# Four key blocks of a pair's scores in one session, and the norm's scale on GpSimd

## The chip, the cores and the metric

The kernel runs on one core of one Trainium2 chip. The metric is the device time of one execution in microseconds; of several runs, the median. A profile comes from one further execution on the chip.

## What is computed

Attention with normalized queries and keys over 8 batches, 12 heads, 448 positions and 64 elements a head, then a mixer on its output: a low-rank mix over the positions (rank 32) and an MLP of width 3072 over 768 channels, each added to its input.

```python
def _attn_ref(q, k, v, g_q, g_k):
    def rmsnorm(x, g):
        rms = np.sqrt(np.mean(x * x, axis=-1, keepdims=True) + 1e-06)
        return x / rms * g
    q_n, k_n = (rmsnorm(q, g_q), rmsnorm(k, g_k))
    scores = np.matmul(q_n, k_n.transpose(0, 1, 3, 2)) / np.sqrt(q.shape[-1])
    scores = scores - np.max(scores, axis=-1, keepdims=True)
    attn = np.exp(scores)
    attn = attn / (np.sum(attn, axis=-1, keepdims=True) + 1e-09)
    return np.matmul(attn, v)

def _moe_ref(x, U, V, w_ch1, w_ch2):
    xt = x.transpose(0, 2, 1)
    h = xt @ U @ V
    u = x + h.transpose(0, 2, 1)
    ch = np.maximum(u @ w_ch1, 0.0) @ w_ch2
    return u + ch
```

The result must agree with this; the matmuls take bf16.

## The kernel before

**Pairs.** Two heads make a pair, and there are 48 pairs, p = 0 to 47, six to a batch. Two pairs make a load (t = p // 2). The 448 positions lie as 112 partitions by four blocks. One step of a pair goes through these stages:

- `load` (L184) brings q and k of a load from HBM, on SP's DMA queue; `load_v` brings v.
- `squares` (L215, POOL) and `reduce` (L218, DVE) give the sums of squares, and `rsqrt` (L223 and L224, ACT: Ln, then Exp with the scale -0.5) turns them into 1/rms. They go to a PSUM bank of their own, `rs_bank`, from which `rs_of(p)` takes 16 columns by p % 6.
- `scale` (L229, DVE) multiplies q and k by 1/rms and writes bf16 `qkn`, of which there are three buffers.
- The scaled pair is turned. Up to pair 11 PE does it (`transposes`, L244), and DVE copies the result out of PSUM. From pair 12 on a DMA on SP's queue does it (`dma_transposes`, L262), and ACT multiplies the gains in afterwards (`gains`, L267).
- `scores(p, kcs)` (L276, PE) takes the four key blocks, kc = 0 to 3. Each is two matmuls of 64 rows by 448 columns, one for each head, on the two halves of the array's rows; they start within a few nanoseconds of each other and write to two PSUM banks. A run of such matmuls with nothing else between is called a session here.
- `expo(p, kc)` (L281, ACT) takes the exponential of one key block of both heads, 112 x 896, from PSUM into SBUF (`E`).
- `values(p, hh)` multiplies `E` by v (L289, 16 matmuls of 65 columns), and DVE divides by the row sum into x.

**Mixer.** `mixing(b)` is the low-rank part: `mix_t` (L336 into `pm`, L345 out of it) and `mix_x` (L359 to L362 into `px`, L364 out of it), then DMA transposes into `u`. `mlp(b)` is a generator. Its first half computes 24 chunks `ph` (L392, six matmuls each), with a relu after each on ACT (L395) or DVE (L397): from batch 1 on, every third chunk is DVE's. Its second half computes `po` (L416, 24 matmuls that add up in one bank), and DVE adds x (L420). Even batches have 384 columns in a chunk `ph`, odd ones 512.

**Order.** A long `head` does the first batch's attention from a list written out by hand (`HEAD`). After it the MLP of batch b is woven with the attention of batch b + 1. `attention(b)` gives a list of pieces, each with a weight; `weave` runs the MLP's generator until the share of its work that the weights ask for is done, then issues the piece. PE, ACT, DVE, POOL and SP's queue each execute in the order in which this issues. Before pair 12 (`early`), `scale(p + 1)` is issued in pair p; from then on `scale(p + 2)`, with its DMA transposition.

**PSUM.** There are eight banks: three for tiles with the tag "mm" (`ph`, `po`, `o`, `px`, `pm`, `pt`), two times two for `sc`, and one for `rs_bank`. A tile of a pool waits for the readers of the one whose bank it takes.

The lines that issue the scores of one pair, in `attention`:

```python
            add(2 if 6 < p <= 12 else 1, scores, p, (0, 1))
            add(0, expo, p, 0)
...
            alone = p >= 12 and p % 6 == 0
            add(0 if alone else 1, expo, p, 1)
...
            add(2 if alone else 1, scores, p, (2, 3))
...
            add(0, expo, p, 2)
...
            add(0 if early else 1, expo, p, 3)
```

Of the kernel before, what the change touches and what calls it, by code (L numbers as in the profile page):

```python
# [9 lines left out]
FP32 = mybir.dt.float32  # L10
BF16 = mybir.dt.bfloat16
AX = mybir.AxisListType.X
AF = mybir.ActivationFunctionType
# [4 lines left out]
def kernel(  # L18
# [13 lines left out]
    nc = tc.nc  # L32
    B, H, S, D = q.shape
# [5 lines left out]
    P = 128  # L39
    NJ = 4  # L40
    SP = S // NJ
# [4 lines left out]
    PAD = 64  # L46
# [15 lines left out]
    consts = ctx.enter_context(tc.tile_pool(name="consts", bufs=1))  # L62
    norm = ctx.enter_context(tc.tile_pool(name="norm", bufs=2))
    upool = ctx.enter_context(tc.tile_pool(name="upool", bufs=1))
    opool = ctx.enter_context(tc.tile_pool(name="opool", bufs=3))
    ps_mm = ctx.enter_context(tc.tile_pool(name="ps_mm", bufs=3, space=bass.MemoryType.PSUM))
    ps_s = ctx.enter_context(tc.tile_pool(name="ps_s", bufs=2, space=bass.MemoryType.PSUM))
    ps_r = ctx.enter_context(tc.tile_pool(name="ps_r", bufs=1, space=bass.MemoryType.PSUM))

    shift = consts.tile([P, 3 * P], BF16, name="shift")  # L70
    ident = shift[:, P:2 * P]
# [16 lines left out]
    NE, NV, NQ, NWARM = 2, 3, 4, 12  # L88
    Es = [consts.tile([SP, 2, PAD + NJ * S + PAD], BF16, name=f"E{i}") for i in range(NE)]
# [7 lines left out]
    qkL = [consts.tile([P, 2, 2, 2, NJ * D], FP32, name=f"qk{i}") for i in range(2)]  # L97
    vL = [consts.tile([P, HG, NJ * D], FP32, name=f"vt{i}") for i in range(2)]

    rs_bank = ps_r.tile([SP, 6 * 16], FP32, name="rs_bank")  # L100

    def rs_of(p, n=1, of=rs_bank):

        c = 16 * (p % 6)
        return of[:, c:c + 16 * n]

    spare = hT.rearrange("p k n -> p (k n)").bitcast(FP32)

# [64 lines left out]
    sqs, qkns, scs, t4s, us, begun = {}, {}, {}, {}, {}, {}  # L173
# [43 lines left out]
    def reduce(p, hs=ALL):  # L217
        nc.vector.tensor_reduce(rs_of(p, of=sums).rearrange("p (s h j) -> p s h j", s=2, h=2)[:, :, hs],  # L218
                                sqs[p].rearrange("p (s h j d) -> p s h j d", s=2, h=2, d=D)[:, :, hs], AX, OP.add)

    def rsqrt(p, n=1):
        rs = rs_of(p, n)
        nc.scalar.activation(rs, rs_of(p, n, sums), AF.Ln, bias=eps)  # L223
        nc.scalar.activation(rs, rs, AF.Exp, scale=-0.5)  # L224

    def scale(p):
        t, a = divmod(p, 2)
        qkns[p] = norm.tile([SP, NJ, 4, D], BF16, tag="qkn", name="qkn", bufs=3)
        nc.vector.tensor_tensor(  # L229
            qkns[p].rearrange("p j g d -> p g j d"),  # L230
            qk_of[t][0:SP, a].rearrange("p s h (j d) -> p (s h) j d", d=D),
            rs_of(p).rearrange("p (g j) -> p g j ()", j=NJ).to_broadcast([SP, 4, NJ, D]),
            OP.mult)

    def k_side(p):

        return qkTs[3] if p == 0 else qkTs[p % NQ]

    def blocks(p):
        return qkTs[p % NQ][:, 0:SQK].rearrange("p (j s r) -> p j s r", j=NJ, s=2)  # L240
# [28 lines left out]
    def scores(p, kcs):  # L269
        flat, n = k_side(p), SP if p == 0 else P  # L270
        for kc in kcs:
            sc = ps_s.tile([P, 2, 512], FP32, tag="s", name="sc")
            c = (2 * kc + 1) * SP
            for hh in range(2):
                pp = slice(hh * D, (hh + 1) * D)
                nc.tensor.matmul(sc[0:n, hh, 0:S], flat[pp, c:c + n], blocks(p)[pp, :, 0],  # L276
                                 start=True, stop=True)
            scs[p, kc] = sc

    def expo(p, kc):  # L280
        nc.scalar.activation(Es[p % NE][:, :, PAD + kc * S:PAD + (kc + 1) * S], scs.pop((p, kc))[0:SP, :, 0:S],  # L281
                             AF.Exp, scale=float(D) ** 0.5)

    def products(p, hh, o):
        par, E, va, hl = p // 6 % 2, Es[p % NE], vas[(p // 2) % NV], 2 * (p % 2) + hh
# [145 lines left out]
    def attention(b):  # L431
        items = []

        def add(weight, fn, *args):
            items.append((weight, lambda: fn(*args)))

        for p in range(b * 6, b * 6 + 6):
            t, odd = divmod(p, 2)
            early = p < 12
            if p == 12:  # L440
                add(0, gains, p)
            add(2 if 6 < p <= 12 else 1, scores, p, (0, 1))
            add(0, expo, p, 0)
            if p == 11:
                add(0, touch, 7)
                add(0, load, 7)
                add(0, load_v, 7)
            elif early and odd:
                add(0, rsqrt, p + 1, 2)
                add(0, scale, p + 1)  # L450
            elif early and p > 6:
                add(0, scale, p + 1)
            elif p >= 12 and p + 2 < NP:
                add(0, scale, p + 2)
                add(0, dma_transposes, p + 2)
            alone = p >= 12 and p % 6 == 0
            add(0 if alone else 1, expo, p, 1)
            if p % 6:
                add(1, values, p - 1, 0)
            if t + 2 < NT:  # L460
                for a in range(2):
                    if odd and p > 11 or p == 11 and a == 0:
                        add(0, reduce, 2 * t + 4 + a if p > 11 else 12)
                    elif not odd and not early:
                        add(0, squares, 2 * t + 4 + a)
            add(2 if alone else 1, scores, p, (2, 3))
            if early and not odd:
                add(0.5, transposes, p + 1)
                if p < 10:
                    add(0, reduce, p + 2)  # L470
            add(0, expo, p, 2)
            if p % 6:
                add(1, values, p - 1, 1)
            if early and not odd:
                if p < 10:
                    add(0, reduce, p + 3)
                for a in range(2):
                    if p != 8:
                        add(0, squares, (10 if p == 6 else 12) + a)
            if odd and p > 11 and t + 3 < NT:  # L480
                add(0, load, t + 3)
                add(0, load_v, t + 3)
            if not odd and t + 1 < NT:
                add(0, cast_v, t + 1)
            if p + 1 < NP and p > 11:
                add(0, gains, p + 1)
            add(0 if early else 1, expo, p, 3)
            if early and odd and p < 11:
                add(1, transposes, p + 1)
            if p == 9:  # L490
                add(0, touch, 6)
                add(0, load, 6)
                add(0, load_v, 6)
            if odd and p > 11 and t + 2 < NT:
                add(0, rsqrt, 2 * t + 4, 2)
        add(1, values, b * 6 + 5, 0)
        add(1, values, b * 6 + 5, 1)
        return items
# [53 lines left out]

    def head():
        warm, rsb = (ps_s.tile([P, 2, 512], FP32, tag="s", name="sc") for _ in range(2))
        banks = [ps_mm.tile([P, 512], FP32, tag="mm", name=f"bank{i}") for i in range(3)]
        held = {}
        copies = {"a": nc.scalar.copy, "v": nc.vector.tensor_copy}
        rs0 = [rs_bank[:, 0:8], rsb[0:SP, 0, 0:8]]
        sums0 = [sums[:, 0:8], sums[:, 8:16]]
        FIRST, REST = slice(0, 1), slice(1, NJ)  # L560

# [11 lines left out]
        def op(name, p, n, how):  # L573
# [45 lines left out]
            elif name in ("Ek", "El"):  # L619
                js = slice(0, NJ) if p else FIRST if name == "Ek" else REST  # L620
                take_k(p, turned(("T" if p else "T" + name[1], p)), copies[how], js)
            elif name == "SC":
                scores(p, (n,))
            elif name == "X":
                expo(p, n)
# [35 lines left out]
        for word in HEAD.split():  # L661
            word, _, how = word.partition(":")
            name = word.rstrip("0123456789")
            digits = word[len(name):]
            p = int(digits[0]) if digits else 0
# [7 lines left out]
    with tc.manual_schedule():  # L673
# [12 lines left out]
        load_v(2)  # L686
        setup()
        head()
        load(5)
        load_w2(0, 2)  # L690
# [5 lines left out]
        for b in range(B):  # L696
            fill = mlp(b)
            if b == 0:
                for _ in range(5):
                    next(fill)  # L700
                transposes(6)
                load_v(5)
                next(fill)
                extra = [(0, lambda i=i, h=h: mix_x(0, i, h)) for i in range(3) for h in range(2)]
                items = attention(1)
                step = len(items) // 7
                for n, x in enumerate(extra):
                    items.insert((n + 1) * step + n, x)
                weave(fill, volume(0) * 0.585, items)
                squares(14)  # L710
                squares(15)
                items = mixing(1)
                items[3:3] = [(0, lambda: reduce(13)), (0, lambda: rsqrt(12, 2))]
                weave(fill, volume(0) * 0.135, items)
                for a in range(2):
                    scale(12 + a)
                    dma_transposes(12 + a)
                for a in range(2):
                    reduce(14 + a)
                rsqrt(14, 2)  # L720
                load(8)
                load_v(8)
            elif b + 1 < B:
                weave(fill, volume(b % 2) * 0.72, attention(b + 1))
                weave(fill, volume(b % 2) * 0.135, mixing(b + 1))
# [32 lines left out]
```

## Time and profile before

| | us |
|---|---|
| median of 3 runs | 588.72 (587.74 to 589.25) |
| the profiled execution | 587.7 |
| its span | 585.9 |
| PE busy in the span | 578.7 |
| PE busy in the first 40 us (head) | 37.25 |
| PE busy in 250 to 320 us | 70.00 of 70 |
| PE busy from 520 us to the end | 62.70 of 66 |

The profile's page gives the busy time of each engine, the chain of work that ended last, and groups of instructions by source line. A line of a group reads: line, engine, operation, what it writes from what it reads, shapes, the number of instructions, then the busy time of all in us and the mean of one in ns, and after the second bar the idle time of the engine before them and what ended it. A line of the timeline reads: start in us, length in us, engine, line, operation, and the number of instructions merged into it. Matmuls overlap, and their ends are modelled, so times between starts say more than a busy share. L276 and the other numbers are lines of the kernel before.

### The profile page before, as it was taken

The page shows a single profiled execution, that of the slowest core. Times are in us where ns is not written, and L with a number is a line of the kernel's source. Part 1 is how long each engine was busy: PE and PEld are TensorE (multiplying, and loading weights), DVE is VectorE, ACT ScalarE, POOL GpSimd, SP SyncE. Part 2 cuts the span into 40 slices and gives each one's busy share as a digit, 9 for nine tenths or more (in the row PEclk, how much of TensorE's full clock was granted, in tenths as well). Part 3 has the DMA queues.
Part 4 walks back from the last instruction along what each step waited for, and adds up shares of the span by engine and source line. Part 5 has one row for each costly group of instructions (what it writes and reads, how often), then busy time and mean ns, then how long its engine had stood idle before and what let it go on. Part 6 is the DMA issues. An engine that isn't in the chain of part 4 may idle for free.

```text
span 585.9 us, 11336 instructions
## 1 busy us (share of the span) xinstructions
PE 578.7 (99%) x4749; PEld 319.3 (54%) x4749; DVE 294.3 (50%) x601; ACT 264.1 (45%) x427; POOL 125.8 (21%) x111
## 2 busy tenths in 40 slices
PE   8999999999999999999999999999999999999997
PEld 3665555445655556444565556544565555554565
DVE  6968767445544557355443656454454452521111
ACT  7966531666206761366511774066630576112200
POOL 5955041423200333031130330302312000000000
PEclk9999999999999999999999999999999999999999
DMA  8999995914543445454154642651454410140011
GB/s 281 277 245 233 204 283 130 293 33 124 152 95 93 116 130 159 101 140 124 43 152 97 153 139 66 168 134 50 140 142 93 63 33 2 41 95 0 1 54 55
DMA packets 108274, 72.26 MB, mean 123 GB/s; under 512 B 56656, under 2 KB 104768, under 8 KB 108224
## 3 DMA queue, kind: packets, MB, share of 16 engines
q1 hardware_dynamic: 96544, 61.50, 40.1%
q0 software_dynamic: 11008, 9.44, 10.0%
q8 instruction: 37, 0.61, 0.4%
q10 hardware_dynamic: 672, 0.61, 0.4%
q14 instruction: 13, 0.11, 0.1%
HBM read 56.78 MB, written 11.01 MB: 116 GB/s over the span
## 4 chain that ended last, share of the span: by engine, by line
PE 94%; DVE 2%; DMA 2%; SPq 0%; issue 0%; ACT 0%; DVEq 0%
PE ph L392 38%; PE po L416 37%; PE o L289 7%; PE sc L276 7%; PE px L362 1%; DMA Vf<-in_moe_V_dram 1%; DMA qk<-in_q_dram 1%; PE bank L289 1%; PE sc L529 1%; SPq L184 0%; DVE osb L420 0%; DVE qkn L229 0%; PE pt L244 0%; DVE sums L218 0%; DVE qkT L248 0%
## 5 line engine op out<-in xcount | busy, mean ns | idle before, releaser
L281 ACT ACTIVATE E<-sc 112x896 bf16<-112x896 f32 x192 | 171.4, 914 | 156.9 <-PE sc L276 156.8
L416 PE MATMUL po<-w2b,hT 128*128 128x384 bf16 (+1 forms) x1368 | 237.8, 323 | 1.0 <-DVE osb L420 0.8
L416 PEld LDWEIGHTS <-hT 128*128 128x128 bf16 x1368 | 128.5, 98 | 88.3 <-issue 11.0
L392 PEld LDWEIGHTS <-w1b 128*128 128x128 bf16 x1128 | 102.7, 98 | 106.2 <-issue 20.3
L215 POOL TENSOR_TENSOR sq<-qk 112x1024 f32<-112x1024 f32 x42 | 79.4, 1894 | 308.6 <-DMA qk<-in_k_dram 223.2
L392 PE MATMUL ph<-uB,w1b 128*128 128x512 bf16 x576 | 132.4, 379 | 0.0
L395 ACT ACTIVATE hT<-ph 128x512 bf16<-128x512 f32 (+1 forms) x122 | 66.8, 547 | 105.6 <-PE ph L392 104.6
L392 PE MATMUL ph<-uA,w1b 128*128 128x384 bf16 x552 | 100.3, 326 | 0.1
L397 DVE TENSOR_SCALAR hT<-ph 128x384 bf16<-128x384 f32 (+1 forms) x66 | 41.1, 622 | 89.8 <-PE ph L392 89.7
L289 PEld LDWEIGHTS <-E 112*128 112x128 bf16 x1536 | 60.8, 98 | 15.4 <-issue 1.9
L289 PE MATMUL o<-va,E 112*128 112x65 bf16 x1344 | 56.9, 194 | 0.0
L229 DVE TENSOR_TENSOR qkn<-qk,rs_bank 112x1024 bf16<-112x1024 f32 x45 | 54.3, 1213 | 3.5 <-ACT rs_bank L224 3.4
L276 PE MATMUL sc<-qkT 64*128 64x448 bf16 x376 | 54.0, 355 | 0.4 <-DVE qkT L251 0.2
L301 DVE RECIPROCAL rec<-o 128x4 f32<-128x4 f32 x84 | 15.2, 181 | 76.2 <-PE o L289 76.0
L218 DVE TENSOR_REDUCE sums<-sq 112x16 f32<-112x1024 f32 x43 | 50.5, 1208 | 0.6 <-ACT gcol L656 0.4
L420 DVE TENSOR_TENSOR osb<-po,xe 128x384 f32<-128x384 f32 x32 | 17.8, 557 | 40.5 <-PE po L416 40.1
L420 DVE TENSOR_TENSOR osb<-po,xo 128x384 f32<-128x384 f32 (+1 forms) x25 | 13.5, 542 | 43.1 <-PE po L416 43.1
L276 PEld LDWEIGHTS <-qkT 64*128 64x128 bf16 (+1 forms) x384 | 12.6, 94 | 32.9 <-issue 26.6
L364 DVE TENSOR_TENSOR xe<-px,xe 128x384 bf16<-128x384 f32 x32 | 17.8, 556 | 14.7 <-PE px L362 9.1
L201 POOL CAST va<-vt 112x1024 bf16<-112x1024 f32 x23 | 23.9, 1043 | 2.5 <-DMA vt<-in_v_dram 1.8
L267 ACT ACTIVATE qkT<-qkT,gg 128x448 bf16<-128x448 bf16 x36 | 23.8, 661 | 0.0
L309 DVE TENSOR_TENSOR xe<-o,rec 64x64 bf16<-64x64 f32 x84 | 18.3, 218 | 0.7
(92 smaller groups left out, 210.9 us busy)
## 6 DMA issues: line engine op xcount, KB each, us to landing
qk<-in_q_dram SPq DMA_DIRECT2D x44, 256.0 KB, 4.3
qk<-in_k_dram SPq DMA_DIRECT2D x44, 256.0 KB, 4.7
vt<-in_v_dram SPq DMA_DIRECT2D x22, 512.0 KB, 5.7
w1b<-in_moe_w_ch_dram POOLq DMA_DIRECT2D x6, 768.0 KB, 20.3
w2b<-in_moe_w_ch_dram POOLq DMA_DIRECT2D x6, 768.0 KB, 33.2
out_dram<-osb SPq DMA_DIRECT2D x7, 336.0 KB, 2.8
out_dram<-osb SPq DMA_DIRECT2D x8, 288.0 KB, 3.0
out_dram<-osb SPq DMA_DIRECT2D x8, 240.0 KB, 2.7
```

What stands on the lines that cost most here:

```text
L201: nc.gpsimd.tensor_copy(vas[t % NV][:, :, :, 0:D], v_of[t][0:SP].rearrange("p h (j d) -> p h j d", d=D))
L215: nc.gpsimd.tensor_tensor(dst, src, src, OP.mult)
L218: nc.vector.tensor_reduce(rs_of(p, of=sums).rearrange("p (s h j) -> p s h j", s=2, h=2)[:, :, hs], sqs[p].rearrange("p (s h j d) -> p s h ...
L229: nc.vector.tensor_tensor(qkns[p].rearrange("p j g d -> p g j d"), qk_of[t][0:SP, a].rearrange("p s h (j d) -> p (s h) j d", d=D), rs_of(p ...
L276: nc.tensor.matmul(sc[0:n, hh, 0:S], flat[pp, c:c + n], blocks(p)[pp, :, 0], start=True, stop=True)
L281: nc.scalar.activation(Es[p % NE][:, :, PAD + kc * S:PAD + (kc + 1) * S], scs.pop((p, kc))[0:SP, :, 0:S], AF.Exp, scale=float(D) ** 0.5)
L289: nc.tensor.matmul(o[:, i, :], E[:, hh, c:c + P], va[:, hl, kc, :], start=(kc == 0), stop=(kc == NJ - 1))
L392: nc.tensor.matmul(ph, w1b[:, dc, hc * P:(hc + 1) * P], u[:, dc, :], start=(dc == 0), stop=(dc == KD - 1))
L395: nc.scalar.activation(hT[:, hc, 0:n], ph, AF.Relu)
L397: nc.vector.tensor_relu(hT[:, hc, 0:n], ph)
L416: nc.tensor.matmul(po, hT[:, hc, i * P:(i + 1) * P], w2b[:, half, hc, w0:w1], start=(hc == 0), stop=(hc == KH - 1))
L420: nc.vector.tensor_add(osb[:, cols], po, xt[i][:, cols])
```

## The change

- `ps_mm` gets a fourth bank, and the pool of `rs_bank` goes. 1/rms lies in an SBUF tile, `rms`; for pairs below 8 it lies in the fourth bank of the head's tiles instead.
- From pair 8 on `scale` runs on GpSimd (POOL) in place of DVE.
- From batch 1 on (pairs 6 to 47) the four key blocks of a pair are issued as one `scores` call. Blocks 1 and 2 keep tiles of two banks from `ps_s`. Blocks 0 and 3 take two single banks each from `ps_mm`, named `sh`, and their exponentials are done for each head by itself (112 x 448).
- The exponentials come in the order 0, 3, 1, 2, and the weights of the pieces change with it.
- The head's list keeps its order; its scores still take one block at a time.

```diff
-    ps_mm = ctx.enter_context(tc.tile_pool(name="ps_mm", bufs=3, space=bass.MemoryType.PSUM))
+    ps_mm = ctx.enter_context(tc.tile_pool(name="ps_mm", bufs=4, space=bass.MemoryType.PSUM))
     ps_s = ctx.enter_context(tc.tile_pool(name="ps_s", bufs=2, space=bass.MemoryType.PSUM))
-    ps_r = ctx.enter_context(tc.tile_pool(name="ps_r", bufs=1, space=bass.MemoryType.PSUM))
...
-    rs_bank = ps_r.tile([SP, 6 * 16], FP32, name="rs_bank")
-
-    def rs_of(p, n=1, of=rs_bank):
+    rms = consts.tile([SP, 6 * 16], FP32, name="rms")
+    banks0 = []
+
+    def rs_of(p, n=1, of=None):
 
         c = 16 * (p % 6)
-        return of[:, c:c + 16 * n]
+        return (of or (banks0[3][0:SP] if p < 8 else rms))[:, c:c + 16 * n]
...
     def scale(p):
...
-        nc.vector.tensor_tensor(
+        (nc.gpsimd if p >= 8 else nc.vector).tensor_tensor(
...
     def scores(p, kcs):
         flat, n = k_side(p), SP if p == 0 else P
         for kc in kcs:
-            sc = ps_s.tile([P, 2, 512], FP32, tag="s", name="sc")
+            if p > 5 and kc in (0, 3):
+                sc = [ps_mm.tile([P, 512], FP32, tag="mm", name="sh") for _ in range(2)]
+            else:
+                sc = ps_s.tile([P, 2, 512], FP32, tag="s", name="sc")
+                sc = [sc[:, 0], sc[:, 1], sc]
...
     def expo(p, kc):
-        nc.scalar.activation(Es[p % NE][:, :, PAD + kc * S:PAD + (kc + 1) * S], scs.pop((p, kc))[0:SP, :, 0:S],
-                             AF.Exp, scale=float(D) ** 0.5)
+        E, sc = Es[p % NE][:, :, PAD + kc * S:PAD + (kc + 1) * S], scs.pop((p, kc))
+        parts = [(E, sc[2][0:SP, :, 0:S])] if len(sc) > 2 else [(E[:, h], sc[h][0:SP, 0:S]) for h in range(2)]
+        for dst, src in parts:
+            nc.scalar.activation(dst, src, AF.Exp, scale=float(D) ** 0.5)
...
-            add(2 if 6 < p <= 12 else 1, scores, p, (0, 1))
+            add(3 if p % 6 == 1 else 2 if 6 < p <= 12 else 1, scores, p, range(NJ))
             add(0, expo, p, 0)
...
-            alone = p >= 12 and p % 6 == 0
-            add(0 if alone else 1, expo, p, 1)
+            add(0, expo, p, 3)
             if p % 6:
                 add(1, values, p - 1, 0)
...
-            add(2 if alone else 1, scores, p, (2, 3))
...
-            add(0, expo, p, 2)
+            add(1, expo, p, 1)
             if p % 6:
                 add(1, values, p - 1, 1)
...
-            add(0 if early else 1, expo, p, 3)
+            add(1, expo, p, 2)
...
-        banks = [ps_mm.tile([P, 512], FP32, tag="mm", name=f"bank{i}") for i in range(3)]
+        banks = banks0
+        banks.extend(ps_mm.tile([P, 512], FP32, tag="mm", name=f"bank{i}") for i in range(4))
...
-        rs0 = [rs_bank[:, 0:8], rsb[0:SP, 0, 0:8]]
+        rs0 = [banks0[3][0:SP, 0:8], rsb[0:SP, 0, 0:8]]
```

## The prediction

> **What bounds the kernel now.** I read the page's busy times and chain first, then the PE timeline around single score sessions, then the groups by form for the price of each evacuation, then the POOL timeline of the first batch.
>
> ```profile
> PE 578.7 (99%) x4749; PEld 319.3 (54%) x4749; DVE 294.3 (50%) x601; ACT 264.1 (45%) x427; POOL 125.8 (21%) x111
> PE 94%; DVE 2%; DMA 2%; SPq 0%; issue 0%; ACT 0%; DVEq 0%
> ```
>
> TensorE is the bound: 99% busy, 94% of the chain. DVE's 50% matters nowhere by itself. So an edit counts only if it changes how long PE takes over its matmuls, or makes PE wait. What a session of scores costs is seen in three places:
>
> ```profile
> 15.48 0.36 PE L276 MATMUL sc<-qkT 64*128 64x448 bf16 x2
> 15.77 0.68 PE L289 MATMUL bank<-va,E 112*128 112x65 bf16 x16
> ...
> 327.60 0.65 PE L392 MATMUL ph<-uA,w1b 128*128 128x384 bf16 x3
> 328.18 0.55 PE L276 MATMUL sc<-qkT 64*128 64x448 bf16 x4
> 328.67 0.50 PE L392 MATMUL ph<-uA,w1b 128*128 128x384 bf16 x2
> ```
>
> From start to start, a session of one key block (two 64-row matmuls at once) takes 0.29 us and one of two blocks 0.49: a block costs 0.19 to 0.20, and leaving the session about 0.10. Three 384-column matmuls take 3 x 0.163 = 0.49 (a run of 12 takes 1.96), yet the session starts 0.58 after them: entering costs about 0.10. So 0.20 us per session lies in the two changes between 64 and 128 rows, while PE counts as busy.
>
> The evacuations' prices, and how they queue on ACT:
>
> ```profile
> L281 ACT ACTIVATE E<-sc 112x896 bf16<-112x896 f32 x192 | 171.4, 914 | 156.9 <-PE sc L276 156.8
> L395 ACT ACTIVATE hT<-ph 128x512 bf16<-128x512 f32 x64 | 38.2, 597 | 78.6 <-PE ph L392 78.5
> L395 ACT ACTIVATE hT<-ph 128x384 bf16<-128x384 f32 x58 | 28.6, 492 | 26.9 <-PE ph L392 26.0 <-POOL sq L215 0.5
> L397 DVE TENSOR_SCALAR hT<-ph 128x512 bf16<-128x512 f32 x32 | 22.1, 692 | 61.6 <-PE ph L392 61.6
> L397 DVE TENSOR_SCALAR hT<-ph 128x384 bf16<-128x384 f32 x34 | 18.9, 556 | 28.2 <-PE ph L392 28.1
> ...
> 328.29 0.49 ACT L395 ACTIVATE hT<-ph 128x384 bf16<-128x384 f32 x1 [1.16 <-PE ph L392]
> 328.67 0.91 ACT L281 ACTIVATE E<-sc 112x896 bf16<-112x896 f32 x1
> ...
> 179.70 1.73 ACT L281 ACTIVATE E<-sc 112x896 bf16<-112x896 f32 x2 [23.42 <-PE sc L276]
> 181.31 1.12 ACT L395 ACTIVATE hT<-ph 128x384 bf16<-128x384 f32 x2
> ```
>
> A relu starts 0.04 us after its last matmul ended (327.60 + 0.65 = 328.25, then 328.29). ACT starts its next instruction before the last one ends: 0.39 after a 384-column relu, 0.80 after an 896-column exponential. In between lies a 448-column exponential: estimates of 0.44 apart and 0.545 from start to end. What PE does with a bank that isn't free is seen at the start of mixing:
>
> ```profile
> 366.58 0.56 DVE L420 TENSOR_TENSOR osb<-po,xe 128x384 f32<-128x384 f32 x1 [0.16 <-PE po L416]
> ...
> 367.19 1.14 PE L416 MATMUL po<-w2b,hT 128*128 128x384 bf16 x6 [0.21 <-DVE osb L420]
> ```
>
> PE stands until the reader ends (367.14) and 0.05 more. Waits of this kind come to under 2 us after the head now.
>
> **What the Trainium skill says.** "TensorEngine Tiling (Array Packing)", Key Properties: changing the tiling mode drains TensorE. The trace agrees, with the 0.10 us at either side. The same page, Gotcha 1: different row tiles write to different PSUM banks, so the two heads of a block need two; they do here, before and after. "PSUM — Partial Sum Buffer", bank collisions: a semaphore is to guard PSUM by bank; so a bank is free when its whole evacuation ended, as in the wait above. "GPSIMD Engine Reference", Engine selection: two-input elementwise work is about twice as slow on GpSimd as on VectorE; the trace has 1894 ns for a two-input 112x1024 on POOL (squares) and 1213 on DVE (scale).
>
> **The change, part by part.**
>
> *Sessions.* The PE order of the changed program has 42 sessions of eight score matmuls (pairs 6 to 47) where there were 84 of four; the head keeps its own. 42 x 0.20 = 8.5 us go.
>
> *The fourth bank for mm tiles.* At four starts of mixing (86.7, 227.0, 366.7, 506.3 us) a new po waited as shown, 0.54 from pm's second column to po against 0.28 where nothing waits: 4 x 0.26 = 1.0 us. In the new order po takes a bank whose reader ended over 1 us before. Short waits after score sessions (0.16 us at 47, 0.08 or 0.09 at five others) fall too: 0.6. Gain so far 10.1.
>
> *Banks inside a session: the added waits.* Key blocks 0 and 3 now take two mm banks each, in the order 0, 1, 2, 3. All eight PSUM banks are needed within 0.9 us, and the program's waits tell which one is late. Take t = 0 at the start of the last matmul before a session. With 384 columns the session starts at 0.26, block 3 at 0.84 and the next work at 1.12 if nothing waits; with 512 at 0.31, 0.89 and 1.18. Two things are later:
>
> Block 3's second head goes to the bank of the MLP chunk just ended, whose relu has only begun: free at 0.33 + 0.04 + 0.49 + 0.05 = 0.90 (ACT) or 0.97 (DVE), with 512 columns 1.07 or 1.16. Then the next chunk goes to the bank of block 0's first head. Its exponential stands behind that relu on ACT: 0.36 + 0.39 = 0.75, end 1.29, free 1.35 (1.50 with 512); with a DVE relu it starts when block 0 is there, free at 1.25. Everything in PE's queue stands behind either wait. Loss of a session: 384 columns 0.13 (DVE relu) or 0.22 (ACT relu); 512 columns 0.27 or 0.33. Where both of the last two relus are ACT's, with 384 columns the previous pair's last exponential (0.80) lies between them and pushes the second back by 0.21: 0.43. Where rsqrt's Ln and Exp (0.42) lie there too: 0.85, with 512 columns 0.75. Where a po accumulates across the session only three mm banks turn: block 3's second head needs block 0's first bank, free at 0.65 + 0.55 + 0.05 = 1.25, and 0.285 later PE goes on: 0.41.
>
> Counted over the orders of PE and ACT: MLPs of batches 2, 4, 6: 2 x 0.22 + 0.13 + 0.43 + 0.85 + 0.41 = 2.26 each, 6.8. Batch 1: 4 x 0.33 + 0.27 + 0.41 = 2.0. Batches 3 and 5: 3 x 0.33 + 2 x 0.41 + 0.75 = 2.55 each, 5.1. Batch 0 (pairs 6 to 11): 0.22, then 0.65 (only three banks, block 0's second head waits for the relu), 0.13, 0.51, and 0.57 twice (three banks, and an mm tile at once on block 0's second bank): 2.65. Sum 16.5 us, a mean of 0.39 per session against the 0.20 that it saves. Bounds: 0.15 if most relus come early, 0.5 if ACT is further behind than I have it.
>
> *Scale on POOL.* The form of L604 (same shape of operands) takes 404 ns for 128 elements and 836 for 384, so 1.69 ns each and an estimate of 1.92 us for 1024; at least DVE's 1.21, at most twice that. POOL's queue is in order, and scale(8) stands behind this:
>
> ```profile
> 50.76 1.90 POOL L215 TENSOR_TENSOR sq<-qk 112x1024 f32<-112x1024 f32 x1 [1.91 <-DVE rec L301]
> 52.60 1.04 POOL L201 CAST va<-vt 112x1024 bf16<-112x1024 f32 x1
> ...
> 52.30 0.56 PE L244 MATMUL pt<-shift,qkn 112*128 112x112 bf16 x8
> ```
>
> The square at 50.76 waits for keys (the name in brackets is the last semaphore; its DVE producer ended at 48.0), so it comes no earlier. scale(8) then runs from 53.6 to 55.5, and PE's transposes of pair 8 wait for it. They were at 52.30; the new order puts one chunk more (0.97) before them, and the sessions of pairs 6 and 7 move them 0.3 later: 53.6. PE stands 1.9 us (1.2 to 2.5). Later early pairs have a microsecond or more in hand, and from pair 12 on a scaled pair has a whole pair (8 us or more) until its gains. The loop that could bite is scale, transpose, load, squares, cast, scale: about 1.9 + 7 + 3.7 + 1.0 = 13.6 us against 16.1 for two pairs in the short MLPs. It fits, so loads on SP come later and nobody waits. DVE's 40 x 1.21 = 48 us less hide nothing that was late. rms in SBUF is needed because POOL reads it; at 32 columns its Ln and Exp cost the same.
>
> *ACT's split.* Four halves at 0.44 instead of two at 0.80: 0.16 us a pair on an engine 45% busy; it is in the session sums.
>
> Sum: -10.1 + 16.5 + 1.9 = +8.3 us. On the profiled execution, 587.7 (span 585.9), that is 596.0; the median of the runs, 588.7, lies 1.0 above it, so 597.0.
>
> **Rivals.**
> 1. *The saved switches win* (the other side, 12%): 8.5 + 1.6 - 1.9 = 8.2 us go, less the waits. The point is a mean wait of 0.20 us per session: below it the kernel is faster; at 0.10 it gains 4.0, giving 584.7. For it: ACT has 55% idle, and half of the relus before sessions might end early. Against: even the cheapest session of the 512-column MLPs comes to 0.27, because the relu is longer than three blocks of scores.
> 2. *It evens out* (10%): waits of 0.20 a session, the 0.43 and 0.85 cases being the first to fall if ACT isn't behind: 588.7.
> 3. *POOL becomes the chain* (8%): scale at twice DVE's time or more, blocked by DVE. At 3.8 us the loop above takes 17.4, 1.3 late in each of nine double pairs of the short MLPs, so 12 us more: about 609. Against: POOL at 21% gets 40 x 1.9 = 76 us more, 34% in all.
>
> **How the numbers follow.** The forecast has 70%: 597, its own range 591 to 602 (sessions at 0.27 to 0.5, POOL's wait at 1.2 to 2.5). A measurement tells about 0.3%, 1.8 us. With the rivals: faster 12%, within 0.3% 10%, slower 78%. The range that leaves no more than 2 in 10 out reaches past the second rival and a little over the forecast's own: 587 to 603.
>
> **What would show it.** PE's span from one session to the next should lengthen by 0.1 to 0.6 us a pair, with idle or stretched gaps before block 3's second head and before the next chunk, released by ACT (hT, E). PE should stand near 54 us on POOL's qkn. The mixing waits should be gone. It is wrong if sessions of 1.12 us are the rule, or if PE waits for qkT.

## The result, and the profile after

The changed kernel takes 597.12 us (median of 4 runs, 595.26 to 599.74) against 588.71 before: a ratio of 1.0148, 95% interval 1.0106 to 1.0190, so 6.2 to 11.2 us more. The prediction said 597.0. One execution of the kernel with more sessions (below) took 616.21 us at a mean granted clock of 0.947 and is left out as a slow one.

The page of the changed kernel: busy times, then the chain that ended last. In the changed kernel the scores stand at L280, the exponentials at L288, the relus at L401 and L403, `ph` at L398 and `po` at L422; L229 is `scale` in both.

```profile
PE 581.5 (98%) x4749; PEld 327.7 (55%) x4749; DVE 247.5 (42%) x561; ACT 267.2 (45%) x511; POOL 200.0 (34%) x151
PE 81%; ACT 10%; DMA 6%; POOL 1%; DVE 1%; issue 1%; SPq 0%; POOLq 0%; ACTq 0%
```

The span grew from 585.9 to 595.9. PE's matmuls are the same, but its share of the chain fell from 94% to 81%, and ACT, which was at 0%, has 10% with the same busy time as before (267 against 264). That is how a bound that has picked up waits looks: the busy shares hardly move, the chain does.

The groups that answer to those shown of before (line, engine, operation, what it writes from what it reads, count; busy us, mean ns; idle before, releaser):

```profile
L229 POOL TENSOR_TENSOR qkn<-qk,rms 112x1024 bf16<-112x1024 f32 x40 | 76.0, 1903 | 230.1 <-issue 220.8
L288 ACT ACTIVATE E<-sc 112x896 bf16<-112x896 f32 x108 | 97.5, 922 | 2.0 <-PE sc L280 1.9
L288 ACT ACTIVATE E<-sh 112x448 bf16<-112x448 f32 x168 | 77.7, 551 | 38.0 <-PE sh L280 38.0
L280 PE MATMUL sh<-qkT 64*128 64x448 bf16 x168 | 39.5, 353 | 2.6 <-ACT hT L401 1.8
```

The scale costs 1903 ns on POOL and the half exponential 551 ns, where the prediction had estimated 1920 and 545. The last line misleads: it puts PE's idle time before `sh` at 2.6 us, while the waits in the sessions sum to 16.7, some 12 of them before an `sh` (worked out below). A matmul's modelled end lies 0.35 us after its start, though the next block may start after 0.19 and the second head of a block at once, so a wait of up to some 0.2 us, or 0.35 before a second head, hides inside "busy". Starts have to be compared.

PE's timeline of the changed kernel for two sessions in the MLP of batch 4, and ACT's for the second:

```profile
326.33 1.14 PE L398 MATMUL ph<-uA,w1b 128*128 128x384 bf16 x6
327.40 0.36 PE L280 MATMUL sh<-qkT 64*128 64x448 bf16 x2
327.60 0.54 PE L280 MATMUL sc<-qkT 64*128 64x448 bf16 x4
327.98 0.41 PE L280 MATMUL sh<-qkT 64*128 64x448 bf16 x2
328.48 0.81 PE L398 MATMUL ph<-uA,w1b 128*128 128x384 bf16 x4
...
340.45 0.36 PE L280 MATMUL sh<-qkT 64*128 64x448 bf16 x2
340.65 0.65 PE L280 MATMUL sc<-qkT 64*128 64x448 bf16 x4
341.12 0.35 PE L280 MATMUL sh<-qkT 64*128 64x448 bf16 x1
341.78 0.35 PE L280 MATMUL sh<-qkT 64*128 64x448 bf16 x1 [0.31 <-ACT hT L401]
342.21 0.65 PE L398 MATMUL ph<-uA,w1b 128*128 128x384 bf16 x3
...
339.97 0.91 ACT L288 ACTIVATE E<-sc 112x896 bf16<-112x896 f32 x1
340.77 0.32 ACT L223 ACTIVATE rms<-sums,eps 112x32 f32<-112x32 f32 x1
341.12 0.23 ACT L224 ACTIVATE rms<-rms 112x32 f32<-112x32 f32 x1
341.26 0.47 ACT L401 ACTIVATE hT<-ph 128x384 bf16<-128x384 f32 x1
```

First session: from its start to the next chunk 1.08 us, against 0.86 if nothing waited, without one nanosecond of marked idle. It is the case with 384 columns and one relu on ACT, priced at 0.22. Second: two heads of block 3, which normally start together, start at 341.12 and 341.78. Before PE can go on, ACT ends an exponential, the Ln and Exp of 1/rms and only then the relu of the last chunk (341.26 + 0.47 = 341.73); PE goes on 0.05 later. That is the dearest case, priced at 0.85; from 340.45 to 342.21 it is 1.76, so 0.90 lost.

POOL's and PE's timeline where the transposes of pair 8 wait for the scale that POOL has taken over:

```profile
53.60 1.89 POOL L215 TENSOR_TENSOR sq<-qk 112x1024 f32<-112x1024 f32 x1 [3.19 <-DMA qk<-in_k_dram]
55.44 1.04 POOL L201 CAST va<-vt 112x1024 bf16<-112x1024 f32 x1
56.44 3.76 POOL L229 TENSOR_TENSOR qkn<-qk,rms 112x1024 bf16<-112x1024 f32 x2
...
55.04 1.14 PE L398 MATMUL ph<-uA,w1b 128*128 128x384 bf16 x6
58.40 0.57 PE L244 MATMUL pt<-shift,qkn 112*128 112x112 bf16 x8 [2.22 <-POOL qkn L229]
```

The square waits for keys, the cast and the scale stand behind it, and PE stands 2.22 us.

The first `po` after `pm`, which waited 0.21 us for `osb` before the change, goes on at once:

```profile
374.97 0.33 PE L342 MATMUL pm<-xo,Ub 128*32 128x384 bf16 x3
375.24 0.99 PE L422 MATMUL po<-w2b,hT 128*128 128x384 bf16 x5
```

**Where the 10.0 us of the profiled span came from.** Cut at the first `ph` of each MLP, the stretches of batches 0 to 6 are longer by 2.61, 0.50, 0.61, 1.25, 0.61, 1.25 and 0.67 us: 7.5 in all. The other 2.5 lie ahead of the first `ph` (40.37 us against 37.89). TensorE's granted clock accounts for most of that. These are windows of 1 us in the head of the changed kernel (columns: us, PE busy and matmuls, granted clock, DMA share, GB/s); in the kernel before the clock is 1.00 in all four windows from 9 to 13 us:

```profile
9.00:10.00 1.00, 1.00 (x11) 0.77 1.08 382
...
12.00:13.00 1.00, 1.00 (x5) 0.53 1.09 381
```

In between it is 0.50. A clock of 0.77 in the first window means half clock from 9.54 on, 0.53 in the last half clock up to 12.94: a stretch of 3.4 us, which costs PE up to 1.7 us of work. The heads of the 14 profiles sort by this: eight without such a stretch take 37.9 to 39.0 us, four with one 39.6 to 40.4, and two with twice its length 40.7 and 41.0. The kernel before has none and the kernel with more sessions has two, with the same head, so the change isn't the cause; what is was not followed up.

**What the clock does to the runs.** One stretch of 3.4 us at half clock lowers the mean clock of an execution by 0.003, and the record has this mean for each. Executions of the kernel before took 587.3 to 588.5 us at 0.999 or 1.0 (15 of 23, those beside the first experiment) and 589.6 to 590.4 at 0.997 (six of them). The changed kernel took 595.26 and 595.94 us at 1.0, and 596.59, 597.05 and 597.66 at 0.997 (this result and the next section). At the same clock it is therefore longer by 7.7 and 7.2 us, which agrees with the 7.5 us of the batches. The rest of its 8.7 us is that its executions had more such stretches: by their clocks some 11 in eight, against 10 in 23.

**A measure for the sessions.** In what follows, the excess of a session is the time from the start of the last matmul before it to the start of the next one after it, less that matmul's own pitch (0.163 us at 384 columns, 0.215 at 512, 0.03 at 65) and less 0.19 per key block. After the head, before has 84 sessions with 17.6 us of excess, 77 of them at 0.20 each. The changed kernel has 42 with 25.1. At 0.20 for the switch of modes, 42 cost 8.4, so 16.7 us are waits.

### The profile page after: what moved, and what is told of

The parts are those of the page before. It is cut to its first block, busy times and chain, and to the rows that moved or that the text cites. A ratio compares the mean times of both kernels' runs of the same rounds, so it can differ in the third digit from the quotient of the medians.

```text
span 595.9 us, 11354 instructions
## 1 busy us (share of the span) xinstructions
PE 581.5 (98%) x4749; PEld 327.7 (55%) x4749; DVE 247.5 (42%) x561; ACT 267.2 (45%) x511; POOL 200.0 (34%) x151
## 4 chain that ended last, share of the span: by engine, by line
PE 81%; ACT 10%; DMA 6%; POOL 1%; DVE 1%; issue 1%; SPq 0%; POOLq 0%; ACTq 0%
PE po L422 37%; PE ph L398 32%; PE o L295 7%; DMA qk<-in_k_dram 6%; ACT E L288 5%; ACT hT L401 3%; PE sh L280 2%; PE px L368 1%; POOL sq L215 1%; PE pm L342 1%; PE sc L518 0%; PE sc L280 0%; POOL qkn L229 0%; PE pt L244 0%; SPq L184 0%
## 5 line engine op out<-in xcount | busy, mean ns | idle before, releaser
L422 PE MATMUL po<-w2b,hT 128*128 128x384 bf16 (+1 forms) x1368 | 235.2, 323 | 0.1
L422 PEld LDWEIGHTS <-hT 128*128 128x128 bf16 x1368 | 129.0, 98 | 85.9 <-issue 7.5
L398 PEld LDWEIGHTS <-w1b 128*128 128x128 bf16 x1128 | 106.6, 97 | 111.1 <-issue 19.1
L401 ACT ACTIVATE hT<-ph 128x512 bf16<-128x512 f32 (+1 forms) x122 | 66.4, 547 | 218.8 <-PE ph L398 218.1
L229 POOL TENSOR_TENSOR qkn<-qk,rms 112x1024 bf16<-112x1024 f32 x40 | 76.0, 1903 | 230.1 <-issue 220.8
L398 PE MATMUL ph<-uB,w1b 128*128 128x512 bf16 x576 | 130.2, 379 | 1.0
L398 PE MATMUL ph<-uA,w1b 128*128 128x384 bf16 x552 | 98.1, 326 | 1.1
L288 ACT ACTIVATE E<-sc 112x896 bf16<-112x896 f32 x108 | 97.5, 922 | 2.0 <-PE sc L280 1.9
L403 DVE TENSOR_SCALAR hT<-ph 128x384 bf16<-128x384 f32 (+1 forms) x66 | 41.0, 621 | 131.4 <-PE ph L398 131.2
L288 ACT ACTIVATE E<-sh 112x448 bf16<-112x448 f32 x168 | 77.7, 551 | 38.0 <-PE sh L280 38.0
L280 PE MATMUL sh<-qkT 64*128 64x448 bf16 x168 | 39.5, 353 | 2.6 <-ACT hT L401 1.8
L280 PEld LDWEIGHTS <-qkT 64*128 64x128 bf16 (+1 forms) x384 | 16.2, 95 | 27.2 <-issue 14.8
L280 PE MATMUL sc<-qkT 64*128 64x448 bf16 x208 | 30.8, 351 | 0.4 <-ACT E L288 0.4
```

The source lines that it names most:

```text
L229: (nc.gpsimd if p >= 8 else nc.vector).tensor_tensor(qkns[p].rearrange("p j g d -> p g j d"), qk_of[t][0:SP, a].rearrange("p s h (j d) -> ...
L280: nc.tensor.matmul(sc[hh][0:n, 0:S], flat[pp, c:c + n], blocks(p)[pp, :, 0], start=True, stop=True)
L288: nc.scalar.activation(dst, src, AF.Exp, scale=float(D) ** 0.5)
L398: nc.tensor.matmul(ph, w1b[:, dc, hc * P:(hc + 1) * P], u[:, dc, :], start=(dc == 0), stop=(dc == KD - 1))
L401: nc.scalar.activation(hT[:, hc, 0:n], ph, AF.Relu)
L403: nc.vector.tensor_relu(hT[:, hc, 0:n], ph)
```

## The experiments

The theory: PE loses to banks inside the longer sessions more than the saved switches are worth, and once to POOL. Rivals: what costs is the load that moved between engines, or a switch of modes is worth less than 0.20 us, or a long session costs of itself.

### The changed kernel again, and with the scale left on VectorE

> The changed kernel once more, beside the others of this group. Theory (waits of the score sessions on evacuations, 16 us, one wait of 1.9 us on POOL, against 10 us saved): 595 to 598 us. The profiled execution of it had a head 2.5 us longer than the one of the kernel before, with a lower granted clock; if that belongs to single executions, the head here is 0 to 3 us longer and everything after it lasts 7.5 us longer than in the kernel before, as there.

Measured: 597.76 us (595.94 to 599.84), ratio 1.0162 [1.0127, 1.0196]. Batches 1 to 6 repeat to 0.02 us. Batch 0 doesn't: +4.16 where the first profile had +2.61.

```diff
-        (nc.gpsimd if p >= 8 else nc.vector).tensor_tensor(
+        nc.vector.tensor_tensor(
```

> The changed kernel with scale on DVE in all pairs. PE's order and banks are those of the changed kernel. Theory: only PE's wait before the transposes of pair 8 goes, 1.9 us, and the sessions keep their waits: about 595.2 if the changed kernel has 597.1. Rival (a lighter DVE evacuates sooner, so POOL is a gain): the sessions' waits grow with DVE's 48 us and it is as slow as the changed kernel or slower. Rival (POOL's chain delays all later pairs): 4 us or more faster.

Measured: 593.20 us (592.94 to 593.91), ratio 1.0082 [1.0055, 1.0108], with 25.04 us of excess in the sessions against 25.08. VectorE has its 40 scales back and no session changes: the load of VectorE plays no part in the waits. Batch 0 is +0.44, so POOL's part is 2.2 us in the one profile and 3.7 in the other. PE's timeline, and below it PE's time in stretches of 1 us, show why, in the second profile of the changed kernel:

```profile
59.12 0.93 PE L244 MATMUL pt<-shift,qkn 112*128 112x112 bf16 x8 [2.29 <-POOL qkn L229]
```

```profile
58.00:59.00 1.00, 0.00 (x0) 1.00 1.31 204
59.00:60.00 1.00, 0.88 (x9) 0.56 1.31 203
60.00:61.00 1.00, 1.00 (x5) 0.50 1.32 204
61.00:62.00 1.00, 1.00 (x6) 0.50 1.30 202
62.00:63.00 1.00, 1.00 (x8) 0.74 1.33 207
```

PE waited 2.29 us here, hardly longer than the 2.22 of the first profile, but then ran at half its clock for over 3 us: 0.44 + 0.50 + 0.50 + 0.26 = 1.7 us of work lost behind the wait. In the first profile the clock stayed at 1.00 behind the wait. "TensorE: Matmul & The Clock Gate", Part 1 of the Trainium skill, says that the clock halves after an idle window of about 3.4 us, and that these windows run free of the program. The length doesn't fit, since 2.29 us of standing still were enough here. The free-running part fits the difference between the two profiles. An estimate: counted on in steps of 3.4 us from the end of the stretch at half clock in the first profile's head (12.94), the edge of a window falls near 57.2, in the middle of its wait from 56.18 to 58.40, so neither window was idle for more than some 1.2 us. In the second profile the half clock begins at 59.12, just where the wait ends, so the whole wait lay in one window. No run moved the wait to test this.

### GpSimd from pair 12 on, and GpSimd alone

Here pairs 8 to 11 keep VectorE, and 36 of 40 scales stay on POOL (the expectation's count of 24 of 28 is wrong).

```diff
-        (nc.gpsimd if p >= 8 else nc.vector).tensor_tensor(
+        (nc.gpsimd if p >= 12 else nc.vector).tensor_tensor(
```

> The changed kernel with the scale on GpSimd only from pair 12 on; pairs 8 to 11, those whose transposes TensorE makes itself, keep it on VectorE. 24 of the 28 GpSimd calls stay. Theory, only the wait before pair 8's transposes costs: the time is that of the changed kernel with every scale on VectorE, 593.2 us (592.5 to 594.2), and batch 0 is longer than before by about 0.4 us, not 2.6 to 4.2. Rival, GpSimd's 1.9 us per scale costs wherever it stands (later pairs late too, or shared ports with VectorE): 595 to 598, as the changed kernel, with batches 1 to 6 each longer than in the run with VectorE.

Measured: 594.87 us (593.19 to 595.24), ratio 1.0097 [1.0079, 1.0115]; batches 0 to 6 at +0.41, 0.50, 0.61, 1.25, 0.61, 1.25, 0.67, those of the version with VectorE to 0.03. The batches speak for the theory, the median lies above it. So both ran once more, on one chip:

> The changed kernel with every scale on VectorE, once more, on one chip with the version that uses GpSimd from pair 12 on; their medians so far (593.2 and 594.9) came from two chips. Theory (GpSimd costs only before pair 8's transposes): the two ratios to before agree within 0.0015, batch by batch as well. Rival (GpSimd costs some 1.7 us in later batches too): this one is lower by 0.003.

> The changed kernel with GpSimd's scale from pair 12 on, on the same chip as the version with every scale on VectorE. Theory: the same time within 0.9 us. Rival: longer by 1.7 us.

Measured: 595.04 us, 1.0102 [1.0084, 1.0121], with VectorE; 593.50, 1.0078 [1.0059, 1.0097], with GpSimd from pair 12. The order is reversed, which neither theory has. The clocks of the executions resolve it. Those at 0.999 or 1.0 took 592.94 to 593.91 us with VectorE (five) and 593.19 to 593.70 with GpSimd from pair 12 (six); those at 0.996 or 0.997 took 594.60 to 595.59 (five) and 594.18 to 595.24 (six). The groups differ in how many they have of each, and GpSimd from pair 12 on costs nothing that can be seen.

The other way round, everything of the change but the long sessions: before with the fourth bank, 1/rms in SBUF and GpSimd from pair 8.

```diff
-    ps_mm = ctx.enter_context(tc.tile_pool(name="ps_mm", bufs=3, space=bass.MemoryType.PSUM))
+    ps_mm = ctx.enter_context(tc.tile_pool(name="ps_mm", bufs=4, space=bass.MemoryType.PSUM))
...
-        nc.vector.tensor_tensor(
+        (nc.gpsimd if p >= 8 else nc.vector).tensor_tensor(
```

> The kernel before (two sessions of two blocks for a pair) with the fourth single bank and 1/rms in SBUF, and the scale on GpSimd from pair 8 on: everything of the change but the merged sessions. Theory: 1.0 us of mixing waits and 0.6 of short ones gone, GpSimd's wait before pair 8's transposes back with 2 to 4.5 us: before plus 0.5 to plus 3, 589 to 591. Rival, GpSimd's wait costs only together with the merged sessions (their transposes are nearer): 587, as the run with the scale left on VectorE.

Measured: 592.45 us (591.40 to 593.29), ratio 1.0062 [1.0043, 1.0081]. The version without GpSimd took 587.37 beside it, so GpSimd costs 5.1 us here, more than with the long sessions. Both expectations miss. PE's timeline in this run, and then its windows of 1 us:

```profile
51.45 1.14 PE L392 MATMUL ph<-uA,w1b 128*128 128x384 bf16 x6
56.21 0.57 PE L244 MATMUL pt<-shift,qkn 112*128 112x112 bf16 x8 [3.63 <-POOL qkn L229]
56.62 3.80 PE L392 MATMUL ph<-uA,w1b 128*128 128x384 bf16 x12
```

```profile
56.00:57.00 1.00, 0.79 (x10) 0.84 1.30 202
57.00:58.00 1.00, 1.00 (x5) 0.50 1.32 206
...
60.00:61.00 1.00, 1.00 (x7) 0.95 1.32 205
```

POOL's chain hangs on the arrival of keys and comes at the same distance from the head, while PE, with one chunk less ahead of the transposes, is there 1.4 us earlier. So it waits 3.63 us, and 12 matmuls then take 3.80 us in place of 2.12 (the length that a view further down shows for 12 at full clock): 3.6 + 1.7 = 5.3, against 5.5 in batch 0 of the two profiles. Both sides matter for the size of a wait, not the late one alone.

### The fourth bank alone

As the last, with the scale on VectorE.

> The kernel before with the fourth single bank and 1/rms in SBUF alone; scale on VectorE, two sessions of two blocks for a pair. Theory: the mixing's four waits of 0.26 us and some 0.6 us of short waits go, nothing is added: 587.1 (586.3 to 588). Rival, the fourth bank was needed by nobody and something else ends last in those places: 588.7, within 0.3% of before either way, so the waits in the trace decide: PE's idle time before the mixing's matmuls.

> The fourth bank and 1/rms in SBUF alone, once more, on the chip of the other run of this call so that the two can be set side by side: 587.4 (586.5 to 588.2).

Measured: 587.37 us (585.73 to 588.22, 21 runs), ratio 0.9969 [0.9960, 0.9978], and 586.70, 0.9959 [0.9945, 0.9973]. PE's timeline at the place of the prediction's example has no wait left:

```profile
366.89 0.33 PE L336 MATMUL pm<-xo,Ub 128*32 128x384 bf16 x3
367.15 1.15 PE L416 MATMUL po<-w2b,hT 128*128 128x384 bf16 x6
```

In the batches 2.0 us are gone (1.7 in the second run): 0.26 or 0.27 in each of batches 2, 4 and 6, the rest, 0.9 to 1.2, in batch 0. Set start against start, batch 0 lost its wait of 0.16 after the session at 47 us, 0.20 before a product of `values` at 66.5, 0.28 at the start of mixing and 0.43 later in it (92.2 and 92.7); the second run has a new wait of 0.29 at 51.2. The five waits of 0.08 or 0.09 after later sessions, which the prediction also counted to the fourth bank, are as long as before.

### More sessions instead of fewer

The kernel before, with every key block asked by itself: 129 sessions after the head instead of 84.

```diff
-            add(2 if 6 < p <= 12 else 1, scores, p, (0, 1))
+            w = 2 if 6 < p <= 12 else 1
+            add(w / 2, scores, p, (0,))
+            add(w / 2, scores, p, (1,))
```

(blocks 2 and 3 in the same way)

> The kernel before with each key block asked for by itself, at half the weight: 45 score sessions more than before, with no further bank taken. Theory (0.20 us for each session, for the two changes of tiling mode): 9.0 us slower than the kernel before, about 597.7. Rival (the gaps at a session's edges are how the records model a matmul's end, and cost nothing): 588.7. More than 600 would mean that single blocks wait for their exponentials too.

Measured: 600.36 us (598.97 to 601.48), ratio 1.0203 [1.0171, 1.0236]; the batches are 10.98 us longer. Of the 129 sessions 119 have an excess of 0.20 us, whatever their length; 45 x 0.20 = 9.0, and ten sessions wait for 2.3 us in all, where seven of before wait for 0.8. So the prediction's price of a switch holds in the other direction too.

### Short exponentials

The changed kernel, with the exponentials of blocks 0 and 3 done for 32 of the 448 columns; the remaining columns of `E` are left out. PE's work is unchanged.

```diff
-        parts = [(E, sc[2][0:SP, :, 0:S])] if len(sc) > 2 else [(E[:, h], sc[h][0:SP, 0:S]) for h in range(2)]
+        parts = [(E, sc[2][0:SP, :, 0:S])] if len(sc) > 2 else [(E[:, h, 0:32], sc[h][0:SP, 0:32]) for h in range(2)]
```

> The changed kernel with the exponentials of key blocks 0 and 3 over 32 of 448 columns; the rest of E for these blocks is left as it was. Each such exponential is then about 0.2 us long instead of 0.545. Theory (the next work waits for block 0's exponential behind the last relu): the sessions' waits fall from 16.5 to about 8, so 8 us faster than the changed kernel, 588 to 590; what remains are the relus. Rival (the time goes elsewhere: weights of the pieces, POOL, the split of the exponentials as such): no more than 2 us faster.

Measured: 589.45 us (587.02 to 591.76, 20 runs), ratio 1.0011 [0.9998, 1.0025]: 8.3 us less than the changed kernel beside it. The excess falls from 25.1 to 16.7. The session of the first view above, in this kernel's PE and ACT timelines:

```profile
320.53 0.36 PE L280 MATMUL sh<-qkT 64*128 64x448 bf16 x2
320.73 0.54 PE L280 MATMUL sc<-qkT 64*128 64x448 bf16 x4
321.11 0.42 PE L280 MATMUL sh<-qkT 64*128 64x448 bf16 x2
321.46 0.82 PE L398 MATMUL ph<-uA,w1b 128*128 128x384 bf16 x4
...
320.64 0.49 ACT L401 ACTIVATE hT<-ph 128x384 bf16<-128x384 f32 x1 [25.83 <-PE ph L398]
321.02 0.28 ACT L288 ACTIVATE E<-sh 112x32 bf16<-112x32 f32 x2
```

From session to chunk it is now 0.93 instead of 1.08. What stays is the relu of the last chunk, for whose bank block 3's second head waits; the wait for block 0's exponential is gone. Over all sessions the changed kernel has some 4 us of waits before the next work and 11.5 between the two heads of block 3; here nothing is left before the next work, and 7.4 between the heads. So 8.4 of the 16.7 us of waits hang on the length of the exponentials of blocks 0 and 3. Where the trace marks the rest, it names the relu (L401) as what ended the wait; no run shortened the relus.

### Sessions of three

If the switch is worth 0.20 us and only the banks eat it, shorter merges ought to gain. Three blocks fit without the last chunk's bank: one block in two single banks, two in the two-bank tiles, so three pairs take four sessions. This is the version with the fourth bank, with such sessions from batch 2 on, 8 to a batch for 12.

```diff
+            three([(p, 0), (p, 1), (p, 2)])
...
+            three([(p, 3), (q, 0), (q, 1)])
...
+            three([(q, 2), (q, 3), (r, 0)])
...
+            three([(r, 1), (r, 2), (r, 3)])
```

> As the run with the fourth bank alone, and from batch 2 on the twelve key blocks of three pairs are asked in four sessions of three, the first block of each in two single banks and the other two in the two-bank tiles: eight sessions in a batch in the place of twelve, none of which needs a bank that the session's own or the last chunk's relu still holds for long. Theory (0.20 us for each session saved, and what the change lost was lost to the banks of a session of four): 24 sessions x 0.20 = 4.8 us less than with the fourth bank alone, 582 (581 to 585). Rival, a longer session costs of itself, whatever its banks, since ScalarE's exponentials then come in bunches that the relus wait behind: no gain or a loss, 587 to 590.

Measured: 595.14 us (594.04 to 596.47), ratio 1.0108 [1.0089, 1.0127]: a miss, and a loss. Of the 48 long sessions 34 lie at 0.20, as a session of three costs in the theory; 14 wait, 11.8 us in all. The greatest of them in PE's and ACT's timelines:

```profile
183.98 0.36 PE L280 MATMUL sh<-qkT 64*128 64x448 bf16 x2
185.82 0.55 PE L280 MATMUL sc<-qkT 64*128 64x448 bf16 x4 [1.48 <-ACT qkT L267]
...
183.50 1.72 ACT L288 ACTIVATE E<-sc 112x896 bf16<-112x896 f32 x2
185.09 0.68 ACT L267 ACTIVATE qkT<-qkT,gg 128x448 bf16<-128x448 bf16 x1
```

A session across two pairs asks for the second pair's keys one chunk after the first pair's last exponentials, and the gains of that pair stood behind these on ACT. Not the length of the session costs, but an input of it that was issued too late. So the order was mended:

```diff
+            if first:
+                add(0, gains, q)
             three([(p, 0), (p, 1), (p, 2)])
...
-            add(0, expo, p, 2)
+            add(1 if first else 0, expo, p, 2)
...
-            pre(r)
             add(1, values, q, 0)
+            pre(r)
```

and the second of two sums on VectorE behind the head's normalizing.

> The run with sessions of three blocks lost time in 12 of its 48 sessions: the second of each batch waited 1.4 to 1.6 us for its gains on ScalarE, which stood last in a queue of exponentials, and the others mostly for o's and ph's banks behind VectorE's sums and scale. Here the second pair's gains are asked before the batch's first session, the first pair's third exponential a chunk later, and one of the two sums and the scale of each third pair behind the heads' normalizing. Nothing is left out. Theory (a longer session costs nothing of itself; only what its banks and gains wait for costs): the waits go, 12 to 9.3 us less than the run before it, four sessions a batch saved at 0.20: 582.6 to 586 us, faster than the fourth bank alone by 1.5 to 4.8. Rival (bunched exponentials delay whatever stands behind them, so waits move on to the next chunk): 588 or more, with PE's idle before ph or po in the place of that before the second session.

Measured: 584.49 us (584.18 to 584.98), ratio 0.9920 [0.9907, 0.9932]; the fourth bank alone had 0.9959 beside it. All 48 long sessions lie at 0.20 us now; the same place in PE's timeline:

```profile
183.88 0.36 PE L280 MATMUL sh<-qkT 64*128 64x448 bf16 x2
184.08 0.54 PE L280 MATMUL sc<-qkT 64*128 64x448 bf16 x4
184.56 2.12 PE L398 MATMUL ph<-uA,w1b 128*128 128x384 bf16 x12
```

It is faster than both kernels. Of the 4.8 us that 24 sessions are worth, the batches got 3.2 to 3.6 against the two profiles of the fourth bank alone, and executions at the same clock (0.996 or 0.997) differ by 3.4. In batch 2 the 180 steps from one matmul of `values` to the next take 6.28 us instead of 5.79: the products now wait for exponentials that come in threes. The rival had that much right.

## Why the prediction was right

- *What bounds*: right. Every microsecond found lies in PE's sequence, and VectorE's 54 us more or less moved nothing.
- *Sessions, -8.5*: right (42 x 0.20 is 8.4). 0.20 us in 77 of 84 sessions before, in 119 of 129 with more sessions, and in 48 of 48 sessions of three.
- *The fourth bank, -1.6*: alone it takes 1.7 to 2.0 us out of the batches. The waits of 0.26 at mixing went as said. Of the 0.6 for short waits after sessions only the 0.16 at 47 us is the bank's; the others stayed with it, and other waits in batch 0 went instead. That the size came out near is luck for this part. In the changed kernel the short waits, 0.8 in all, went with the sessions that had them.
- *Banks inside a session, +16.5*: 16.7 measured. The cheap cases with 384 columns came out to 0.01 us: the session at 327.40 lost 0.22, with the relu on ACT, as worked out. The one with rsqrt lost 0.90 for 0.85, mainly because Ln and Exp took 0.49 us on ACT (340.77 to 341.26) and not 0.42: with 1/rms in SBUF they do not "cost the same", but 323 and 229 ns in the mean in place of 292 and 174. For half of the 16.7 the cause is shown by a run (the exponentials of blocks 0 and 3, shortened); that the other half hangs on the relus is read from the traces, and no run undid it.
- *Scale on POOL, +1.9*: the place and the mechanism are right, and the wait of 2.22 us lies in the step's range (1.2 to 2.5). At a clock of 0.999 or 1.0 the changed kernel takes 595.6 us in the mean and the one with VectorE 593.4, which is the wait alone. It is larger than 1.9 because the square that waits for keys began 13.23 us after the first `ph`, and 12.87 in the profile from which it was worked out. What the step left out is what PE may do after a wait: in the second profile half clock cost 1.7 us more. The ratios, 1.0148 and 1.0162 against 1.0082 and 1.0102, differ by 3.7 us (0.0063 x 588.7), but stretches at half clock in the head, as in the first profile, are part of that.
- *ACT's split, and VectorE's 48 us less*: right, both in the sums and nowhere else.
- *The sum*, +8.3: 7.5 in the batches of the first profile, and 7.2 to 7.7 at the same clock. Waits in sessions 16.7, POOL 2.2, switches -8.4, short waits -0.8; what is then missing to 7.5 is -2.2, of which 1.1 went at the starts of mixing. So the forecast was 0.8 too high, in the main because the gains put at 1.6 came to 3.0. That the median still lies 0.1 us from 597.0 is luck: the executions lost different amounts of clock, and range from 595.3 to 599.7.
- *Rivals*: the first needs a mean wait under 0.20 us a session; it was 16.7 / 42 = 0.40. The second would have needed 0.20, too. The third needs the loop over POOL to be late; with 36 scales on POOL nothing shows of it. Its 17.4 us didn't follow from its own terms either: the loop of 13.6 names two scales and counts one, and with that one at 3.8 it is 15.5, under the 16.1 that it had.

## What to carry to other kernels

Before merging two stretches of work to save a fixed price per stretch, count the buffers that the merged one needs at once, and set the saving against the time by which the latest of them comes free: here 0.20 us against 0.40. Where the merge is good, stop it at the length that the free buffers carry, and then follow every input of the longer stretch back through its queue; sessions of three were 6.4 us slower than before with one input issued late (and two less important pieces in its way) and 4.7 faster with them in order. A short wait of TensorE may cost more than its length.

## What the runs showed of the hardware

- TensorE's clock fell to 0.50 for 3.4 us after waits of 2.29 and 3.63 us, and did not after one of 2.22.
- 1/rms in SBUF made ACT's Ln and Exp of it slower: 323 and 229 ns for 32 columns in the changed kernel, 292 and 174 in the kernel before. The one such pair of instructions that still writes to a PSUM bank in the changed kernel takes 292 and 174.
- 1/rms in SBUF made VectorE's own scale slower. The groups of before, and of the version with the fourth bank alone:

```profile
L229 DVE TENSOR_TENSOR qkn<-qk,rs_bank 112x1024 bf16<-112x1024 f32 x45 | 54.3, 1213 | 3.5 <-ACT rs_bank L224 3.4
```

```profile
L229 DVE TENSOR_TENSOR qkn<-qk,rms 112x1024 bf16<-112x1024 f32 x40 | 57.5, 1441 | 4.0 <-ACT rms L224 3.7
L201 POOL CAST va<-vt 112x1024 bf16<-112x1024 f32 x23 | 29.8, 1298 | 2.0 <-DMA vt<-in_v_dram 2.0
```

The median of these scales is still 1.22 us, but the slowest takes 2.85, and POOL's casts went from 1043 to 1298 ns. The Trainium skill, "GPSIMD Engine Reference", Specifications, says that GpSimd shares its SBUF interfaces with VectorE, with contention where an instruction of VectorE has two inputs in SBUF. With 1/rms in PSUM the scale had one. The casts bear it out: in the changed kernel, where 1/rms lies in SBUF too but POOL does the scale, they take 1043 ns again, and 1041 with the scale on POOL from pair 12 on. The slow scales fit it, though no run took GpSimd's work away to show that side. PE waited for none of them.
